# Gated linear attention with a mixer and an MLP on one core: loading two batches in token pairs and replanning the start

## The chip, the cores and the metric

The kernel runs on one core of one Trainium2 chip. The metric is the device time of one execution in microseconds (us); three runs of the kernel before gave 181.0, 179.39 and 182.18 us, a median of 181.0. Lower is better. The core's engines are TensorE (PE in the profile; its weight loads are PEld), VectorE (DVE), ScalarE (ACT), GpSimd (POOL) and SyncE (SP), which here issues every DMA.

## The reference

Two parts follow each other. The first is a recurrence over 768 tokens, for 4 batches and 8 heads of width 48; the second, `_moe_ref`, mixes tokens by a low-rank product and applies an MLP of 384 to 1536 to 384:

```python
def _attn_ref(q, k, v, alpha) -> np.ndarray:
    ...
    for t in range(S):
        state = alpha[:, :, t, :, None] * state + np.einsum('bhd,bhe->bhde', k[:, :, t], v[:, :, t])
        y[:, :, t] = np.einsum('bhd,bhde->bhe', q[:, :, t], state)
    return y.astype(np.float32)
...
    xt = x.transpose(0, 2, 1)
    h = xt @ U @ V
    u = x + h.transpose(0, 2, 1)
    ch = np.maximum(u @ w_ch1, 0.0) @ w_ch2
    return (u + ch).astype(np.float32)
```

x is the recurrence's output with the 8 heads side by side (384 columns). U is 768x32, V 32x768. All inputs and the output are fp32.

## The kernel before, in words

Each batch is cut into six chunks of 128 tokens; a chunk with all 8 heads is called a unit here. A unit needs four loads (alpha, k, q, v), each a tile `io` of 128 tokens x 8 heads x 48 fp32 values, 192 KB. In memory the 48 values of a head and a token stand alone, so such a load consists of pieces of 192 bytes (line 316).

`stage_gla` computes a unit. ScalarE takes the logarithm of alpha (`lt`, line 331). PE sums it over the tokens with a triangular matrix (`f_cum`, 338 to 341), which also gives each column's total. ScalarE exponentiates the sums: `ai` (negative, 349), `aa` (350), `tot` (351). k is multiplied by `ai` (`rk`) and q by `aa` (`rq`, both 356, on VectorE or GpSimd). PE transposes both (368) and an engine copies them out of PSUM as `kt` and `qt` (379, 380). PE forms the scores, two heads at a time on the two halves of its rows (`f_sc`, 389), VectorE masks them (`pm`, 399). `f_d` (414, 416) multiplies `rk` with `rv`, the bf16 copy of v, to the change of the state; `st` is the new state (427, from batch 1 on by way of `sm`, 439). `f_y` (450, 452) adds what the old state and the masked scores give, and a copy writes it to `xb` (458).

`stage_mix` follows when the six chunks of a batch are there: `utx` = x transposed times U (469), its product with V (500) added to x as `ub` (501), and the transposed sum `uT` (488 and 491 in batch 0, 510 later). `mlp1` (537) and `mlp2` (560) are the MLP, 72 matmuls each per batch; `h1t` is the hidden layer after the maximum (547, 549), `ou` the sum that is stored (567, 568). The weights come in 24 loads and are cast to bf16 as `w_sb` (294, 295); rows are whole, 1536 bytes apiece.

The order of all work is made by `Plan.run` before the kernel is built. It keeps a clock for each engine, knows a cost in ns for each operation on each engine that can do it, and takes again and again the operation that can start first; among those that are ready within 1 ns the lowest `prio` wins. For loads it keeps a second clock, `dma`: each load adds its cost there, and its data count as landed 1600 ns later. Buffers come from pools (36 `io` tiles, 8 PSUM banks). An operation of the MLP may take a bank only if `reserve` others are free. The order is then fixed: every engine runs its own list, and an instruction that waits holds up all that stand behind it on that engine. In its early part PE also gets filler matmuls (268) until `warm_until`.

Priorities order the loads: unit number plus 0.0 for alpha, 0.1 for k, 0.2 for q, 1.25 for v (0.3 in the last unit); w1 at 5.5, that is behind the last loads of batch 0, and w2 at 7.9. The call in the last lines is `for b ... for c: st = stage_gla(b, c, st, xb)`, then the mix and the MLP of the batch.

## Time and profile before

| What | Value |
|---|---|
| median of three runs | 181.0 us (179.39 to 182.18) |
| the profiled execution's own time | 180.75 us |
| its span in the profile | 178.9 us |
| mean granted clock of TensorE | 0.981 |
| read from memory, written | 23.79 MB, 4.72 MB |
| DMA packets, those under 512 bytes | 107603, 101408 |

The page gives busy shares of the whole span; the answers by stretch and the timeline give the same for a part. In a timeline row stand the start and the length in us, the engine, the line, the operation with what it writes and reads, and in brackets the idle time of the engine before it with what ended it. In the chain of waits a row is a piece of the path that ended last: start, length, engine and line. A group row ends with its total busy time and the mean ns of one.

### The profile page before, as it was taken

The page shows a single profiled execution, that of the slowest core. Times are in us where ns is not written, and L with a number is a line of the kernel's source. Part 1 is how long each engine was busy: PE and PEld are TensorE (multiplying, and loading weights), DVE is VectorE, ACT ScalarE, POOL GpSimd, SP SyncE. Part 2 cuts the span into 40 slices and gives each one's busy share as a digit, 9 for nine tenths or more (in the row PEclk, how much of TensorE's full clock was granted, in tenths as well). Part 3 has the DMA queues.
Part 4 walks back from the last instruction along what each step waited for, and adds up shares of the span by engine and source line. Part 5 has one row for each costly group of instructions (what it writes and reads, how often), then busy time and mean ns, then how long its engine had stood idle before and what let it go on. Part 6 is the DMA issues. An engine that isn't in the chain of part 4 may idle for free.

```text
span 178.9 us, 4283 instructions
## 1 busy us (share of the span) xinstructions
PE 164.3 (92%) x1622; PEld 101.9 (57%) x1622; DVE 107.4 (60%) x209; ACT 103.0 (58%) x241; POOL 57.1 (32%) x90
## 2 busy tenths in 40 slices
PE   6878797999989997958999999999999999999992
PEld 2344445566557675535766576566664665666660
DVE  2486678888637895873889699386573722100321
ACT  4557366986775546783879758218867200897000
POOL 5432221226334564606673636425600000000000
PEclk9999799999999999996999999999999999999999
DMA  6999999999999999999999999941000023100222
GB/s 122 221 213 191 195 229 302 261 226 292 309 211 196 232 239 223 232 178 196 219 193 200 208 183 234 196 150 48 0 0 4 0 88 129 50 0 0 88 88 88
DMA packets 107603, 28.77 MB, mean 161 GB/s; under 512 B 101408, under 2 KB 107552, under 8 KB 107584
## 3 DMA queue, kind: packets, MB, share of 16 engines
q1 hardware_dynamic: 107584, 28.52, 69.9%
q8 instruction: 12, 0.20, 0.4%
q14 instruction: 7, 0.06, 0.1%
HBM read 23.79 MB, written 4.72 MB: 159 GB/s over the span
## 4 chain that ended last, share of the span: by engine, by line
PE 65%; DVE 7%; DMA 7%; SPq 6%; POOL 5%; issue 5%; ACT 2%; POOLq 0%; DVEq 0%; ACTq 0%
PE ps L560 24%; PE ps L537 21%; SPq L316 6%; PE ps L368 5%; DMA io<-in_q_dram 3%; DVE pm L399 3%; DMA io<-in_moe_w_ch_dram 2%; POOL rk L356 2%; PE ps L389 2%; PE ps L452 2%; POOL rq L356 2%; PE ps L338 2%; DMA out_dram<-ou 2%; PE ps L500 1%; PE ps L450 1%
## 5 line engine op out<-in xcount | busy, mean ns | idle before, releaser
L537 PE MATMUL ps<-uT,w_sb 128*128 128x384 bf16 x288 | 53.8, 332 | 0.4 <-ACT uT L275 0.4
L560 PE MATMUL ps<-w_sb,h1t 128*128 128x384 bf16 x288 | 50.1, 326 | 0.0
L547 ACT ACTIVATE h1t<-ps 128x384 bf16<-128x384 f32 x70 | 33.4, 490 | 21.8 <-PE ps L537 21.4
L560 PEld LDWEIGHTS <-h1t 128*128 128x128 bf16 x288 | 27.1, 98 | 16.5
L537 PEld LDWEIGHTS <-w_sb 128*128 128x128 bf16 x288 | 26.5, 99 | 16.4 <-issue 1.7
L399 DVE TENSOR_TENSOR pm<-ps,maskc 128x512 bf16<-128x512 f32 x48 | 31.0, 683 | 3.2 <-PE ps L389 3.1
L567 DVE TENSOR_TENSOR ou<-ub,ps 128x384 f32<-128x384 bf16 x24 | 13.3, 553 | 32.7 <-PE ps L560 32.6
L356 POOL TENSOR_TENSOR rk<-io,ai 128x384 bf16<-128x384 f32 x21 | 19.5, 928 | 26.1 <-ACT ai L349 25.0
L549 DVE TENSOR_SCALAR h1t<-ps 128x384 bf16<-128x384 f32 x26 | 13.8, 554 | 8.2 <-PE ps L537 8.2
L356 POOL TENSOR_TENSOR rq<-io,aa 128x384 bf16<-128x384 f32 x16 | 14.6, 914 | 8.5 <-ACT tot L351 5.3
L349 ACT ACTIVATE ai<-ps 128x384 bf16<-128x384 f32 x24 | 12.0, 502 | 8.2 <-PE ps L341 7.6
L331 ACT ACTIVATE lt<-io 128x384 bf16<-128x384 f32 x24 | 12.8, 533 | 4.2 <-DMA io<-in_alpha_dram 4.1
L279 POOL CAST rv<-io 128x384 bf16<-128x384 f32 x18 | 9.6, 540 | 11.7 <-DMA io<-in_v_dram 11.7
L268 PE MATMUL ps<-filler 128*128 128x512 bf16 x34 | 12.2, 471 | 1.2 <-DVE offd L235 1.2
L501 DVE TENSOR_TENSOR ub<-xb,ps 128x384 bf16<-128x384 bf16 x24 | 11.6, 547 | 2.6 <-PE ps L500 2.6
L350 ACT ACTIVATE aa<-ps 128x384 bf16<-128x384 f32 x24 | 12.1, 504 | 0.0
L368 PE MATMUL ps<-ident,rq 128*128 128x128 bf16 x96 | 9.4, 220 | 2.3 <-POOL rq L356 2.0
L368 PE MATMUL ps<-ident,rk 128*128 128x128 bf16 x96 | 9.4, 220 | 2.2 <-POOL rk L356 1.3
L275 ACT CAST xb<-ps 128x384 bf16<-128x384 f32 x16 | 7.7, 479 | 6.1 <-PE ps L452 6.0
L427 POOL TENSOR_TENSOR st<-sm,tot 128x384 bf16<-128x384 f32 x8 | 6.6, 828 | 14.3 <-DVE sm L439 14.3
L452 PE MATMUL ps<-rv,pm 128*128 128x48 bf16 x192 | 9.6, 186 | 1.6 <-DVE pm L399 1.6
L275 ACT COPY qt<-ps 128x512 bf16<-128x512 bf16 x12 | 7.1, 588 | 6.2 <-PE ps L368 6.2
(71 smaller groups left out, 198.7 us busy)
## 6 DMA issues: line engine op xcount, KB each, us to landing
io<-in_alpha_dram SPq DMA_DIRECT2D x24, 192.0 KB, 3.8
io<-in_k_dram SPq DMA_DIRECT2D x24, 192.0 KB, 3.9
io<-in_q_dram SPq DMA_DIRECT2D x24, 192.0 KB, 3.7
io<-in_v_dram SPq DMA_DIRECT2D x24, 192.0 KB, 3.7
io<-in_moe_w_ch_dram SPq DMA_DIRECT2D x24, 192.0 KB, 4.7
out_dram<-ou SPq DMA_DIRECT2D x24, 192.0 KB, 1.9
u_in<-in_moe_U_dram SPq DMA_DIRECT2D x1, 96.0 KB, 3.6
v_in<-in_moe_V_dram SPq DMA_DIRECT2D x1, 96.0 KB, 3.3
```

Source lines behind the costliest of these rows:

```text
L268: P.warm = lambda: nc.tensor.matmul(ps[:, 7, :], lhsT=filler[:, 0:128], rhs=filler, start=True, stop=True)
L275: nc.scalar.copy(dst, src)
L331: P.add({"ACT": 435}, lambda e: nc.scalar.activation(lt()[:, :, 0:D], at(), AF.Ln), r=[at], w=[lt], prio=pr + 40, slack=sl)
L356: eng.tensor_tensor(dst()[:, :, 0:D], a(), x(), op=ALU.mult)
L368: nc.tensor.matmul(t[:, p, :], lhsT=ring()[:, 2 * p : 2 * p + 2, :].rearrange("t h w -> t (h w)"), rhs=ident, start=True, stop=True, is_tr ...
L399: nc.vector.tensor_tensor(pm()[:, :, par, :], s2, maskc.to_broadcast([C, HP, C]), op=ALU.mult)
L452: nc.tensor.matmul(y[:, h * D : (h + 1) * D], lhsT=pm()[:, h // 2, h % 2, :], rhs=rv()[:, h, :], start=(h == 0 and sprev is None), stop=(h ...
L537: nc.tensor.matmul(hb()[:, 0:TW], lhsT=w1_sb[:, ct, jt * 128 : (jt + 1) * 128], rhs=uT()[:, ct, tt * TW : (tt + 1) * TW], start=(ct == 0), ...
L547: nc.scalar.activation(dst, hb()[:, 0:TW], AF.Relu)
L549: nc.vector.tensor_scalar_max(dst, hb()[:, 0:TW], 0.0)
L560: nc.tensor.matmul(hb()[:, 0:DM], lhsT=h1()[:, jt, c * C : (c + 1) * C], rhs=w2_sb[:, jt, :], start=(jt == 0), stop=(jt == NJ - 1),)
L567: P.add({"DVE": 468}, lambda e: nc.vector.tensor_tensor(ou(), ub()[:, c, :], hb()[:, 0:DM], op=ALU.add), r=[hb, (ub, c)], w=[ou], prio=-100)
```

## The change

For batches 0 and 1 (`PAIR`) `stage_pair` takes the place of `stage_gla`. A unit there is half of the heads (4) over 256 tokens, with tokens 2p and 2p + 1 in partition p. A load moves the same 192 KB, in pieces of two tokens, 384 bytes. The unit's lower and upper 64 partitions hold 128 consecutive tokens each (c = 0, 1 in the code). The running sums need two more matmuls (`below`, `upto`), since a partition holds an even token and an odd one. Scores, state and output are formed for each half of the partitions alone: 16 score matmuls of 64x128 for 8, 8 state matmuls for 4, 16 output matmuls on 64 rows for 8. State, `sm` and `xb` operations are half as wide and twice as many. The copy to `qt` writes every second element. Two states run side by side, one for each half of the heads.

Alpha's priority is lowered by 0.7, so that it stands ahead of the unit before it in part; in batches 2 and 3 v comes with its unit. The planner takes 750 ns for a paired load and 1000 for another, a landing time of 2000 ns plus 400 for loads, and lets an operation choose only among engines on which it would end within 150 ns of the earliest. Only GpSimd casts w1. Batch 0's `ub` sums are put behind the start of its MLP. The MLP leaves 1 bank free where it left 4. There is a third `aa` and `ai` tile, new constants are made at the start (`upto`, `below`, `mask2`, `maskp`, `onesel`), and fillers end at 28000 ns in the plan.

The core of the diff:

```diff
-    LAT = {"PE": 215.0, "ACT": 155.0, "DVE": 145.0, "POOL": 110.0, "SP": 0.0}
+    LAT = {"PE": 215.0, "ACT": 155.0, "DVE": 145.0, "POOL": 110.0, "SP": 400.0}
     SWITCH = 95.0
+    TOL = 150.0
...
-                for eng in op.engs:
-                    per.setdefault(eng, []).append((max(t, clock.get(eng, 0.0)), op))
+                at = {eng: max(t, clock.get(eng, 0.0)) for eng in op.engs}
+                soon = min(at[eng] + c for eng, c in op.engs.items()) + self.TOL
+                for eng, c in op.engs.items():
+                    if at[eng] + c <= soon:
+                        per.setdefault(eng, []).append((at[eng], op))
...
-                end = dma + 1600.0
+                end = dma + 2000.0
...
+    PAIR = (0, 1)
+    RES = (1, 1, 1, 0)
...
+    upto = const.tile([C, C], BF16, name="upto")
+    nc.vector.tensor_copy(upto, ut_ones)
+    nc.vector.memset(upto[0:64, 64:128], 0.0)
+    below = const.tile([C, C], BF16, name="below")
+    nc.vector.tensor_tensor(below, upto, ident, op=ALU.subtract)
+    mask2 = const.tile([C, 2, 2 * C], BF16, name="mask2")
+    nc.gpsimd.memset(mask2, 0.0)
+    nc.gpsimd.affine_select(
+        out=mask2, in_=mask2, compare_op=ALU.is_gt, fill=1.0, base=0, pattern=[[1, 2], [-1, 2 * C]], channel_multiplier=2
+    )
+    maskp = const.tile([C, 1, 2, C], BF16, name="maskp")
+    nc.vector.tensor_copy(maskp[0:64, 0], mask2[0:64, :, 0:C])
+    nc.vector.tensor_copy(maskp[64:128, 0], mask2[64:128, :, C : 2 * C])
...
-    aas = Pool(slots("aa", 2, [C, H, D], BF16))
-    ais = Pool(slots("ai", 2, [C, H, D], BF16))
+    aas = Pool(slots("aa", 3, [C, H, D], BF16))
+    ais = Pool(slots("ai", 3, [C, H, D], BF16))
...
-    P.warm_until = 33000.0
+    P.warm_until = 28000.0
...
-    def weight(dst, src, key, prio, pr):
+    def weight(dst, src, key, prio, pr, engs):
         t = Buf(io)
-        P.add({"SP": 560.0}, lambda e: nc.sync.dma_start(flat(t), src), w=[t], prio=prio)
-        P.add({"POOL": 485, "ACT": 435}, lambda e: copy(e, dst, flat(t)), r=[t], w=[key], prio=pr)
+        P.add({"SP": 540.0}, lambda e: nc.sync.dma_start(flat(t), src), w=[t], prio=prio)
+        P.add(engs, lambda e: copy(e, dst, flat(t)), r=[t], w=[key], prio=pr)
...
+                weight(w1_sb[:, ct, cs], moe_w_ch1[ct * 128 : (ct + 1) * 128, cs], ("w1", g, ct), 5.5 + 0.01 * g, 560 + g, {"POOL": 485})
...
+            weight(w2_sb[:, jt, :], moe_w_ch2[jt * 128 : (jt + 1) * 128, :], ("w2", jt), W2AT + 0.001 * jt, 700 + jt, {"POOL": 485, "ACT": 435})
...
     def stage_loads(b):
         def load(t, src, c, key):
+            if b in PAIR:
+                hs, sl = slice((c % 2) * HP, (c % 2 + 1) * HP), slice((c // 2) * 2 * C, (c // 2 + 1) * 2 * C)
+                P.add(
+                    {"SP": 750.0},
+                    lambda e: nc.sync.dma_start(
+                        t().rearrange("p (h j) d -> p h (j d)", j=2), src[b, hs, sl, :].rearrange("h (p j) d -> p h (j d)", j=2)
+                    ),
+                    w=[t], prio=key,
+                )
+                return
             sl = slice(c * C, (c + 1) * C)
-            P.add({"SP": 1020.0}, lambda e: nc.sync.dma_start(t(), src[b, :, sl, :].rearrange("h t d -> t h d")), w=[t], prio=key)
+            P.add({"SP": 1000.0}, lambda e: nc.sync.dma_start(t(), src[b, :, sl, :].rearrange("h t d -> t h d")), w=[t], prio=key)
 
         for c in range(NC):
             at, qt, kt, vt = (Buf(io) for _ in range(4))
             tiles[b, c] = at, qt, kt, vt
             kk = b * NC + c
-            for t, src, o in ((at, alpha, 0.0), (kt, k, 0.1), (qt, q, 0.2), (vt, v, 1.25 if c < NC - 1 else 0.3)):
+            for t, src, o in ((at, alpha, -0.7 if c else 0.0), (kt, k, 0.1), (qt, q, 0.2), (vt, v, 1.25 if c < NC - 1 and b in PAIR else 0.3)):
...
+    def stage_pair(b, u, sprev, xb):
+
+        blk, half = u // 2, u % 2
+        pr = (b * NC + u) * 100.0
+        sl = 0.0 if b == 0 else 150.0
+        at, qt, kt, vt = tiles[b, u]
+
+        def raw(t):
+            return t().rearrange("p (h j) d -> p j h d", j=2)
+
+        def jh(x):
+            return x.rearrange("p (j h) d -> p j h d", j=2)
+
+        lt = Buf(lts)
+        P.add({"ACT": 435}, lambda e: nc.scalar.activation(jh(lt()[:, :, 0:D]), raw(at), AF.Ln), r=[at], w=[lt], prio=pr + 40, slack=sl)
+        rv = Buf(rvs)
+        P.add({"POOL": 480, "ACT": 420}, lambda e: copy(e, jh(rv()), raw(vt)), r=[vt], w=[rv], prio=pr + 20, slack=sl)
+
+        cb = Buf(bank)
...
+        def f_cum(e):
+            l2 = jh(lt()[:, :, 0:D])
+            nc.tensor.matmul(cb()[:, 0:DM].rearrange("p (i h d) -> p i h d", i=2, d=D), lhsT=upto, rhs=l2[:, 0:1].to_broadcast([C, 2, HP, D]), start=True, stop=False)
+            nc.tensor.matmul(cb()[:, 0:Q], lhsT=below, rhs=l2[:, 1], start=False, stop=False)
+            nc.tensor.matmul(cb()[:, Q : 2 * Q], lhsT=upto, rhs=l2[:, 1], start=False, stop=False)
+            nc.tensor.matmul(cb()[:, DM : DM + 8], lhsT=ident, rhs=offd.rearrange("p a b -> p (a b)"), start=False, stop=False)
+            tot4 = cb()[:, DM : DM + 8].rearrange("p (c a b) -> p c a b", c=2, a=2)
+            for a in range(2):
+                for j in range(2):
+                    nc.tensor.matmul(
+                        tot4[:, :, a, :], lhsT=lt()[:, HP * j + 2 * a : HP * j + 2 * a + 2, :].rearrange("t h w -> t (h w)"),
+                        rhs=onesel, start=False, stop=(a == 1 and j == 1),
+                    )
+
+        P.add({"PE": mm(DM, Q, Q, 8, 4, 4, 4, 4)}, f_cum, r=[lt], w=[cb], prio=pr + 30, slack=sl)
...
+        rq, rk = Buf(rqs), Buf(rks)
+
+        def f_scale(e, dst, a, x):
+            eng = nc.gpsimd if e == "POOL" else nc.vector
+            eng.tensor_tensor(jh(dst()[:, :, 0:D]), raw(a), jh(x()), op=ALU.mult)
+
+        both = {"DVE": 420, "POOL": 885}
...
+        def f_sc(e):
+            for n in range(4):
+                a, j = n // 2, n % 2
+                for par in range(2):
+                    o = 64 * par
+                    for c in range(2):
+                        r = slice(64 * c, 64 * c + 64)
+                        nc.tensor.matmul(
+                            sc[par]()[r, n * C : (n + 1) * C],
+                            lhsT=kT()[o : o + D, n, r], rhs=qT()[o : o + D, 2 * a + c, :],
+                            start=(n == 0), stop=(n == 3), skip_group_check=True,
+                        )
+
+        P.add({"PE": mm(*[C] * 4)}, f_sc, r=[kT, qT], w=[sc[0], sc[1]], prio=pr + 10, mode="Q", slack=sl)
+
+        def f_mask(par):
+            s2 = sc[par]().rearrange("p (a j c) -> p a j c", a=2, j=2)
...
+        onpe = b == 0
+        nch = 2 if blk < 2 else 1
+        db = [Buf(bank) for _ in range(nch)]
+        st = Buf(sts)
+        before = [(sprev, 1) if sprev is not None else None, (st, 0)]
+
+        def sview(x):
+            return x[0]()[:, 2 * x[1] : 2 * x[1] + 2, :].rearrange("p a d -> p (a d)")
+
+        def f_id(e, c, last):
+            nc.tensor.matmul(db[c]()[:, 0 : 2 * Q // 2], lhsT=ident, rhs=sview(before[c]), start=not last, stop=last, skip_group_check=True)
+
+        def f_d(e):
+            for n in range(4):
+                a, j = n // 2, n % 2
+                for c in range(nch):
+                    r = slice(64 * c, 64 * c + 64)
+                    more = onpe and c == 1
+                    nc.tensor.matmul(
+                        db[c]()[:, a * 2 * D : (a + 1) * 2 * D],
+                        lhsT=rk()[r, HP * j + 2 * a : HP * j + 2 * a + 2, :].rearrange("t h w -> t (h w)"),
+                        rhs=rv()[r, HP * j + 2 * a : HP * j + 2 * a + 2, :].rearrange("t h d -> t (h d)"),
+                        start=(n == 0 and not (onpe and c == 0 and sprev is not None)), stop=(n == 3 and not more), skip_group_check=True,
+                    )
+
+        if onpe and sprev is not None:
+            P.add({"PE": mm(Q)}, lambda e: f_id(e, 0, False), r=[(sprev, 1)], w=[db[0]], prio=pr + 8, slack=sl)
...
+        yb = Buf(bank), Buf(bank)
+
+        def f_yi(e, c):
+            s = before[c]
+            for a in range(2):
+                nc.tensor.matmul(
+                    yb[c]()[:, 2 * a * D : (2 * a + 2) * D], lhsT=qT()[:, 2 * a + c, :], rhs=s[0]()[:, 2 * s[1] + a, :],
+                    start=(a == 0), stop=False, skip_group_check=True,
+                )
+
+        def f_y(e):
+            for c in range(2):
+                if before[c] is not None:
+                    f_yi(e, c)
+            for h in range(HP):
+                for j in range(2):
+                    for c in range(2):
+                        r = slice(64 * c, 64 * c + 64)
+                        nc.tensor.matmul(
+                            yb[c]()[:, h * D : (h + 1) * D], lhsT=pm()[r, (h // 2) * 2 + j, h % 2, :], rhs=rv()[r, HP * j + h, :],
+                            start=(h == 0 and j == 0 and before[c] is None), stop=(h == HP - 1 and j == 1), skip_group_check=True,
+                        )
+
+        P.add({"PE": mm(*[2 * D] * 4, *[D] * 8) + 95}, f_y, r=[qT, rv, (pm, 0), (pm, 1)] + [x for x in before if x is not None], w=[yb[0], yb[1]], prio=pr, mode="H", slack=sl)
+        for c in range(2):
+            P.add({"ACT": 250, "DVE": 265}, lambda e, c=c: copy(e, xb()[:, 2 * blk + c, half * Q : (half + 1) * Q], yb[c]()[:, 0:Q]), r=[yb[c]], w=[(xb, 2 * blk + c, half)], prio=pr, slack=sl)
+        return st
...
-        both = {"DVE": 420, "POOL": 885} if b <= 1 else {"POOL": 885}
+        both = {"POOL": 885}
```

What the planner makes of it is seen in the engines' lists. On SyncE (names: `io` is the tile that a load fills, `in_..._dram` the input), the fourth alpha and what stands around it, before:

```order
L316 DMA io_105<-in_q_dram 128x8x48
L316 DMA io_106<-in_v_dram 128x8x48
L282 DMA u_in<-in_moe_U_dram 128x6x32
L283 DMA v_in<-in_moe_V_dram 32x768
L316 DMA io_107<-in_alpha_dram 128x8x48
L316 DMA io_108<-in_k_dram 128x8x48
```

and now:

```order
L342 DMA io_121<-in_q_dram 128x4x96
L342 DMA io_122<-in_v_dram 128x4x96
L342 DMA io_123<-in_alpha_dram 128x4x96
L305 DMA u_in<-in_moe_U_dram 128x6x32
L306 DMA v_in<-in_moe_V_dram 32x768
L342 DMA io_124<-in_k_dram 128x4x96
```

Alpha went ahead of U and V, and the pieces became 96 values long. Further on SyncE, the end of batch 1's loads and the first stores of results (`out_dram`), before:

```order
L316 DMA io_125<-in_q_dram 128x8x48
L568 DMA out_dram<-ou_194 128x384
L316 DMA io_126<-in_v_dram 128x8x48
L316 DMA io_127<-in_alpha_dram 128x8x48
L316 DMA io_128<-in_k_dram 128x8x48
L568 DMA out_dram<-ou_195 128x384
L316 DMA io_129<-in_q_dram 128x8x48
L316 DMA io_130<-in_v_dram 128x8x48
L316 DMA io_131<-in_v_dram 128x8x48
```

and now, with loads of batch 2 (the rows of line 349) between them:

```order
L342 DMA io_146<-in_v_dram 128x4x96
L342 DMA io_147<-in_v_dram 128x4x96
L349 DMA io_112<-in_alpha_dram 128x8x48
L349 DMA io_113<-in_k_dram 128x8x48
L349 DMA io_114<-in_q_dram 128x8x48
L349 DMA io_115<-in_v_dram 128x8x48
L349 DMA io_119<-in_alpha_dram 128x8x48
L349 DMA io_117<-in_k_dram 128x8x48
L349 DMA io_120<-in_q_dram 128x8x48
L349 DMA io_122<-in_v_dram 128x8x48
L780 DMA out_dram<-ou_213 128x384
```

The first store, which stood six loads ahead of the end of batch 1's, now stands behind two whole units of batch 2. On PE, the running sums of the first unit (`lt` is the logarithm of alpha, `ps` the PSUM), before:

```order
L338 LDWEIGHTS ut_ones
L338 MATMUL ps<-lt_132,ut_ones 128x384
L339 LDWEIGHTS ident
L339 MATMUL ps<-offd,ident 128x8
L341 LDWEIGHTS lt_132
L341 MATMUL ps<-ones,lt_132 128x2
```

and now:

```order
L384 LDWEIGHTS upto
L384 MATMUL ps<-lt_148,upto 128x384
L385 LDWEIGHTS below
L385 MATMUL ps<-lt_148,below 128x192
L386 LDWEIGHTS upto
L386 MATMUL ps<-lt_148,upto 128x192
L387 LDWEIGHTS ident
L387 MATMUL ps<-offd,ident 128x8
```

Two matmuls of 192 columns came in; each piece still loads its own weights.

107 lines of the change are left out of this document (83 added, 24 removed).

## The prediction, on record before the change was timed

> **What bounds the kernel now.** I read the page first, then busy time by stretch, then the chain of waits, then the timeline of the first 35 us. The page has the span and TensorE's share:
>
> ```profile
> span 178.9 us, 4283 instructions
> PE 164.3 (92%) x1622; PEld 101.9 (57%) x1622; DVE 107.4 (60%) x209; ACT 103.0 (58%) x241; POOL 57.1 (32%) x90
> ```
>
> 92% is an average over stretches with different limits. Busy time by stretch (columns: stretch, its length, then PE, PEld, DVE, ACT and POOL busy, PE clock, DMA share, GB/s):
>
> ```profile
> 5.00:15.00 10.00, 8.20 (x101) 4.62 (x99) 6.98 (x14) 5.63 (x16) 4.77 (x6) 1.00 1.09 215
> 15.00:27.00 12.00, 10.04 (x107) 5.11 (x103) 8.96 (x17) 6.72 (x19) 2.41 (x3) 0.86 1.00 205
> 27.00:34.20 7.20, 6.01 (x75) 3.77 (x76) 5.48 (x11) 5.72 (x13) 0.51 (x2) 1.00 0.98 306
> ...
> 70.20:91.00 20.80, 17.39 (x211) 11.60 (x211) 14.68 (x29) 14.89 (x37) 11.36 (x15) 0.92 1.04 213
> 91.00:112.50 21.50, 21.21 (x259) 14.17 (x258) 18.67 (x34) 15.73 (x39) 11.97 (x17) 1.00 1.02 202
> 112.50:175.50 63.00, 62.83 (x498) 38.60 (x496) 23.96 (x46) 28.42 (x61) 7.25 (x10) 1.00 0.19 60
> ```
>
> The DMA engines are full until 112.5 us, and then nearly idle while PE runs alone. So early on loads set the pace, and later PE's backlog does. To size the backlog I price PE's work from the chain of waits (start us, us, what), in its dense parts:
>
> ```profile
> 61.75 0.45 PE ps L368 x8
> ...
> 62.85 0.17 PE ps L416 x4
> 63.02 0.17 PE ps L450 x4
> 63.19 0.20 PE ps L452 x8
> 63.39 0.33 PE ps L389 x8
> 63.72 0.27 PE ps L338
> ...
> 64.09 2.62 PE ps L560 x16
> ```
>
> One unit (128 tokens, all heads) costs 0.45 transposes + 0.17 state + 0.17 and 0.20 output + 0.33 scores + 0.37 running sums (63.72 to 64.09) = 1.69 us. The MLP and the mixer:
>
> ```profile
> 102.12 0.43 PE ps L469 x6
> 103.70 0.97 PE ps L500 x6
> ...
> 112.47 3.90 PE ps L560 x24
> ...
> 140.67 0.34 PE ps L510 x6
> ...
> 152.06 11.70 PE ps L537 x72
> 163.75 11.71 PE ps L560 x72
> 175.49 0.55 DVE ou L567
> ```
>
> An MLP matmul is 11.70/72 = 0.1626 us, a mix 0.43 + 0.97 + 3 x 0.34 = 2.42. From the first L500 of batch 0 (34.16, below) PE owes 576 MLP matmuls (93.7), 18 units (30.4, less 1.0 for the missing first and last state pieces), 0.97 and three mixes (7.3): **131.3 us**. It takes 175.49 - 34.16 = 141.3, so 10.0 us are not work. Check: from 112.47 the order holds 332 MLP matmuls (54.0) and 8.3 of other pieces, 62.3 in 63.0 us: 1.2% over. The rest of the 10.0 lies mostly in 70.2 to 91, where PE's queue stood behind late loads:
>
> ```profile
> 80.50 0.51 POOL L279 CAST rv<-io 128x384 bf16<-128x384 f32 x1 [4.73 <-DMA io<-in_v_dram]
> 81.06 0.44 PE L416 MATMUL ps<-rv,rk 128*128 128x96 bf16 x4 [2.02 <-POOL rv L279]
> ```
>
> So: front 34.2 + work 131.3 + waits 10.0 + end 3.4 (175.49 to 178.9), and 1.85 around the span, is 180.75, the profiled execution's time. The median shown is 181.0, so nothing has to be scaled.
>
> **Loads.** A 196,608-byte load at 215 and 205 GB/s takes 0.91 and 0.96 us, say 0.94; this is 1024 packets of 192 B on 16 engines, 14.7 ns each. The stretch of weight loads (306 GB/s, 1536-B packets) gives 0.64 us a load, 80 ns a packet. The line through both is 5.3 ns + 0.049 ns a byte: a 384-B packet takes 24.1 ns and a load of 512 of them 0.77 us, 0.17 saved (an estimate). Bounds: 0.94 if time goes by bytes, 0.47 if by packets. I take 0.77, the nearest the rows allow. 24 loads save 4.1 us, all 48 save 8.2. The Trainium skill ("DMA: Bandwidth & Descriptors", Specifications) gives 512 B as the least transfer for full rate; by it 384 B stays in the penalised class. That is the third rival below.
>
> **Front.** The rows are of the last unit of batch 0, and of the load two units earlier:
>
> ```profile
> 12.62 5.37 DMA io<-in_q_dram
> ```
> ```profile
> 26.84 0.90 DVE L356 TENSOR_TENSOR rq<-io,aa 128x384 bf16<-128x384 f32 x1
> 29.53 1.28 DVE L399 TENSOR_TENSOR pm<-ps,maskc 128x512 bf16<-128x512 f32 x2
> 30.87 0.35 PE L452 MATMUL ps<-rv,pm 128*128 128x48 bf16 x7 [0.40 <-DVE pm L399]
> 34.16 1.14 PE L500 MATMUL ps<-utx,vm_sb 128*128 128x384 bf16 x6
> ```
>
> The fourth q landed at 12.62 + 5.37 = 17.99; the sixth comes 8 loads later, 25.5. In the change 22 loads stand up to it, so it lands 22 x 0.17 = 3.7 earlier, at 21.8. With alpha sent a unit ahead, its decay factors are ready by then, where before rq began at 26.84, 1.3 after q. From rq to the end of the output is 26.84 to 31.22 = 4.4, with the strided copy 0.1 more: 26.4; and 2.9 from there to 34.16: MLP start 29.3. VectorE is the doubt. Its forms now (mean ns):
>
> ```profile
> L399 DVE TENSOR_TENSOR pm<-ps,maskc 128x512 bf16<-128x512 f32 x48 | 31.0, 683 | 3.2 <-PE ps L389 3.1
> L356 DVE TENSOR_TENSOR rq<-io,aa 128x384 bf16<-128x384 f32 x8 | 6.7, 832 | 0.3 <-issue 0.3
> L277 DVE COPY kt<-ps 128x512 bf16<-128x512 bf16 x13 | 5.5, 424 | 2.7 <-PE ps L368 2.2
> L427 DVE TENSOR_TENSOR st<-ps,tot 128x384 bf16<-128x384 f32 x8 | 4.4, 553 | 2.0 <-PE ps L416 1.9
> L356 DVE TENSOR_TENSOR rk<-io,ai 128x384 bf16<-128x384 f32 x3 | 1.7, 558 | 5.5 <-ACT ai L349 5.5
> ```
>
> Up to batch 0's last output it now holds 12 pm (7.7 at the 0.64 spacing of the 1.28 row), 8 rk or rq (4.5 to 6.7), 3 copies (1.3), 15 half-width st and xb (between 4.1 at half of 553 and 8.3 at all of it): 17.6 to 24.0 in the 21 us from 5.3. At the lower half that is about 90% full, so I add 0.9: MLP start 30.2, **-4.0**. The extra constants on VectorE and GpSimd (small memsets, a 128x512 mask) run before the first load's factors are wanted and cost 0 to 0.5 there, hidden by the later loads.
>
> **PE work.** Per paired unit: the running sums get 384 more columns (+0.16, by the MLP matmul). Output matmuls go from 8 to 16 on half the rows; the 8 of L452 take 0.20, 25 ns each, so +0.20. Scores: 16 small ones at 25 ns are 0.40 against 0.33, +0.07; upper end, 16 at the 41 ns of the present 8, +0.33. State 8 for 4, +0.03, upper +0.17. Sum +0.46, between 0.16 and 0.86; six units of batch 1: **+2.8** (1.0 to 5.2). Those of batch 0 lie in the front, under the loads. L469 shows that matmuls on column strips do run together: six of 384 columns in 0.43, where L500's six take 0.97. The Trainium skill ("TensorEngine Tiling (Array Packing)", Restrictions and Gotchas) says that column tiling gives up fast weight loading; by it the scores, with 16 weight loads, go to the upper end, and the sum would be 1.6 us more. L469 has only six loads behind long matmuls and can't show it.
>
> **Waits.** Three rows place the DMA limit:
>
> ```profile
> 55.38 2.20 SPq L568 DMA_DIRECT2D out_dram<-ou  x1
> 65.64 1.28 POOL L279 CAST rv<-io 128x384 bf16<-128x384 f32 x2
> 75.94 0.33 PE L416 MATMUL ps<-rv,rk 128*128 128x96 bf16 x4
> ```
>
> Batch 1's last v are there by 65.64. Less 8.2 for 48 loads and 1.3 for two stores that the order now places later, 56.1; four loads of batch 2 (3.8) and a cast (0.5): its first state matmul, at 75.94 before, can run at about 60.5 to 61. (SyncE also stood 2.20 us at a store amid batch 1's loads; the first store now follows them.) PE gets there at 30.2 + 134.1 - 104.5 (work still left there: 44 + 432 MLP matmuls 77.4, three mixes 7.3, the other pieces 19.8) = 59.8, so it loses about 1 us, and then runs on backlog: 61 + 104.5 x 1.012 + 1 + 3.4 + 1.85 = 173.0, a second way to nearly the same time. Waits: 1.2% of 134.1 (1.6), 0.8 at that point, 2 for the other engines in the denser 30 to 75 us: 4.4 for 10.0, **-5.6**. GpSimd alone casting w1 costs 12 x 0.51:
>
> ```profile
> L279 POOL CAST w_sb<-io 128x384 bf16<-128x384 f32 x9 | 4.6, 511 | 10.6 <-DMA io<-in_moe_w_ch_dram 10.4
> L275 ACT CAST w_sb<-io 128x384 bf16<-128x384 f32 x15 | 7.5, 512 | 2.8 <-DMA io<-in_moe_w_ch_dram 2.8
> ```
>
> That is under the 0.64 at which they land, so nothing; what queues behind is batch 1's first rv cast, whose v lands after the last w1 anyway. The choice by end time changes engines, not the amount of work: 0, with +-1 in the range.
>
> **Sum:** 180.75 - 4.0 + 2.8 - 5.6 = 174.0.
>
> **Rivals.** (1) *VectorE becomes the front's limit*: at its upper 24.0 the last pm ends at 29.3, the output 0.4 later and the MLP starts at 32.6; then 32.6 + 134.1 x 1.012 + 2 + 5.25 = 175.6. For: 90% full already. Against: half-width should cost about half. (2) *Half-array matmuls don't overlap*: outputs too at 41 ns (+0.46), all upper ends, 1.1 a unit: 6.7 for 2.8, 177.9, less the 0.8 that PE waits anyway: 177. Against: L389's two halves overlap today. (3) *A 384-B packet costs by its bytes*, the page's rule: no load is shorter, the front has only the fuller VectorE (+0.8), the 10.0 of waits stay, the work is 2.8 more: 184; with the stores' 1.3 and the earlier order 181. Slower. It decides if a paired load takes over 0.9. Against: weight packets run at 306 GB/s, so some cost is per packet. (4) *In-order queues*: the rewritten order holds PE behind one late engine after another and the waits stay 10.0: 179.6. For: DVE, ACT and POOL together are busy 41 of 62 us in 70 to 91 already.
>
> **Chances.** Forecast 0.52 (own range 171 to 176.5), (1) 0.10, (2) 0.12, (3) 0.11, (4) 0.15. A measurement here tells 2% from no change: 177.4 and 184.6. Faster: forecast, (1) and nearly half of (2), 0.67; slower: the upper half of (3) and mishaps, 0.09; same 0.24. The range 170 to 181.5 leaves out most of (3) and a quicker packet.
>
> **What would show it.** Paired loads at 250 GB/s or more in 5 to 20 us (step 1; 215 would be rival 3); the first MLP matmul at 29 to 31; VectorE at 9 tenths before; a paired unit 0.4 to 0.5 dearer on PE; the first state matmul of batch 2 near 61; no slice of 70 to 91 with PE under 9 tenths; the last load landing near 106 and PE dense from 62. Wrong if the MLP starts after 33, or PE waits over 7 us behind that.

## The result, and the profile after

The changed kernel takes **174.5 us** (median of 4 runs, 173.7 to 175.4) against 181.5 for the kernel before in the same comparison (179.4 to 182.2): a ratio of 0.966, 95% interval 0.955 to 0.976. Ratios here and below leave out runs over 1.5% above the fastest of the same kernel, so they are not quite the quotients of the medians. The prediction was 174.0, in a range of 170 to 181.5, with "faster" at 0.67. Time and direction are right. Of the reasons one is missing, and the experiments found it.

The profiled execution took 174.75 us. Its page:

```profile
span 173.0 us, 4823 instructions
...
PE 161.9 (94%) x1862; PEld 104.2 (60%) x1862; DVE 109.0 (63%) x232; ACT 104.1 (60%) x247; POOL 59.5 (34%) x97
```

PE has 240 more instructions in a span that is 5.9 us shorter, and its share goes from 92 to 94%. Busy time by stretch (stretch, its length, PE, PEld, DVE, ACT, POOL, PE clock, DMA share, GB/s):

```profile
5.00:15.00 10.00, 8.26 (x145) 5.30 (x144) 7.57 (x24) 7.97 (x20) 3.60 (x6) 1.00 1.21 262
15.00:27.00 12.00, 10.90 (x212) 7.88 (x212) 9.53 (x22) 8.52 (x23) 6.88 (x11) 0.86 1.04 270
...
50.00:55.00 5.00, 3.54 (x56) 2.52 (x55) 3.83 (x12) 3.15 (x9) 1.42 (x2) 1.00 1.04 232
55.00:90.00 35.00, 35.00 (x466) 23.70 (x463) 27.88 (x56) 24.84 (x60) 17.33 (x23) 1.00 1.03 204
90.00:110.00 20.00, 19.37 (x222) 13.01 (x221) 13.71 (x27) 12.96 (x34) 9.13 (x13) 1.00 1.19 206
110.00:169.50 59.50, 59.50 (x495) 37.14 (x492) 25.55 (x47) 28.26 (x61) 6.63 (x8) 1.00 0.14 48
```

In the front the loads now run at 262 and 270 GB/s (215 and 205 before). From 55 us PE is full, where before 70 to 91 was the thin stretch (17.39 of 20.80); what is left of the waits shows at 50 to 55. The first mixer and MLP matmuls, and the last sum, on the timelines of PE and VectorE:

```profile
30.53 0.33 PE L712 MATMUL ps<-utx,vm_sb 128*128 128x384 bf16 x1
30.69 1.14 PE L749 MATMUL ps<-uT,w_sb 128*128 128x384 bf16 x6
```
```profile
169.54 0.55 DVE L779 TENSOR_TENSOR ou<-ub,ps 128x384 f32<-128x384 bf16 x1 [1.40 <-PE ps L772]
```

So the front ends at 30.5 (34.2 before), 139.0 us follow to the last sum (141.3), then 3.5 of span and 1.75 around it.

Two of the three longest waits of PE behind the front, on the timelines of PE, GpSimd, ScalarE and PE again:

```profile
54.01 0.35 PE L479 MATMUL ps<-rv,rk 64*128 64x96 bf16 x8 [1.46 <-POOL rv L302]
```
```profile
53.45 0.50 POOL L302 CAST rv<-io 128x384 bf16<-128x384 f32 x1 [1.72 <-DMA io<-in_v_dram]
```
```profile
90.41 0.52 ACT L547 ACTIVATE lt<-io 128x384 bf16<-128x384 f32 x1 [1.40 <-DMA io<-in_alpha_dram]
```
```profile
91.46 0.40 PE L605 MATMUL ps<-qt,kt 48*128 48x128 bf16 x8 [0.63 <-ACT qt L298]
```

In the first, a state matmul of batch 1 stands in PE's queue until a v has landed and been cast. In the second ScalarE waits for an alpha, and PE waits 0.63 us for the qt copy queued behind it.

### The profile page after: what moved, and what is told of

It is laid out like the page before. It is cut to its first block, busy times and chain, and to the rows that moved or that the text cites. A ratio compares the mean times of both kernels' runs of the same rounds, so it can differ in the third digit from the quotient of the medians.

```text
span 173.0 us, 4823 instructions
## 1 busy us (share of the span) xinstructions
PE 161.9 (94%) x1862; PEld 104.2 (60%) x1862; DVE 109.0 (63%) x232; ACT 104.1 (60%) x247; POOL 59.5 (34%) x97
## 4 chain that ended last, share of the span: by engine, by line
PE 60%; DMA 19%; SPq 15%; issue 2%; POOL 1%; ACT 1%; DVE 0%; ACTq 0%; POOLq 0%
PE ps L772 27%; PE ps L749 16%; SPq L342 10%; DMA io<-in_v_dram 8%; DMA io<-in_moe_w_ch_dram 5%; SPq L317 3%; DMA io<-in_alpha_dram 3%; PE ps L584 3%; DMA io<-in_k_dram 3%; PE ps L605 2%; PE ps L712 2%; PE ps L722 2%; PE ps L664 1%; PE ps L554 1%; PE ps L418 1%
## 5 line engine op out<-in xcount | busy, mean ns | idle before, releaser
L749 PE MATMUL ps<-uT,w_sb 128*128 128x384 bf16 x288 | 53.1, 326 | 0.0
L772 PE MATMUL ps<-w_sb,h1t 128*128 128x384 bf16 x288 | 52.8, 326 | 0.0
L772 PEld LDWEIGHTS <-h1t 128*128 128x128 bf16 x288 | 26.1, 98 | 16.0 <-issue 1.0
L749 PEld LDWEIGHTS <-w_sb 128*128 128x128 bf16 x288 | 26.1, 98 | 15.4
L615 DVE TENSOR_TENSOR pm<-ps,maskc 128x512 bf16<-128x512 f32 x24 | 15.7, 685 | 6.7 <-PE ps L605 6.5
L572 POOL TENSOR_TENSOR rk<-io,ai 128x384 bf16<-128x384 f32 x12 | 11.0, 916 | 20.2 <-ACT ai L565 18.7
L456 DVE TENSOR_TENSOR pm<-ps,maskp 128x512 bf16<-128x512 f32 x24 | 15.8, 681 | 0.7 <-ACT h1t L759 0.5
L298 ACT CAST xb<-ps 128x192 bf16<-128x192 f32 (+1 forms) x23 | 8.8, 392 | 11.6 <-PE ps L664 7.6
L298 ACT COPY kt<-ps 128x512 bf16<-128x512 bf16 x17 | 10.0, 586 | 5.8 <-PE ps L584 5.3
L298 ACT COPY qt<-ps 128x512 bf16<-128x512 bf16 x17 | 11.3, 663 | 1.6 <-PE ps L418 1.0
L302 POOL CAST w_sb<-io 128x384 bf16<-128x384 f32 x21 | 10.8, 527 | 3.8 <-DMA io<-in_moe_w_ch_dram 3.5
L572 POOL TENSOR_TENSOR rq<-io,aa 128x384 bf16<-128x384 f32 x12 | 11.6, 967 | 0.0
L298 ACT COPY uT<-ps 128x768 bf16<-128x768 bf16 x4 | 3.2, 799 | 8.6 <-PE ps L722 5.1
```

What stands on the lines that cost most here:

```text
L298: nc.scalar.copy(dst, src)
L302: nc.gpsimd.tensor_copy(dst, src)
L456: nc.vector.tensor_tensor(dst, s2, maskp.to_broadcast([C, 2, 2, C]), op=ALU.mult)
L572: eng.tensor_tensor(dst()[:, :, 0:D], a(), x(), op=ALU.mult)
L615: nc.vector.tensor_tensor(pm()[:, :, par, :], s2, maskc.to_broadcast([C, HP, C]), op=ALU.mult)
L749: nc.tensor.matmul(hb()[:, 0:TW], lhsT=w1_sb[:, ct, jt * 128 : (jt + 1) * 128], rhs=uT()[:, ct, tt * TW : (tt + 1) * TW], start=(ct == 0), ...
```

## The experiments

Twelve kernels ran, in four sets, each set on one chip beside runs of the kernel before, whose median in these sets was 183.3 to 183.5. Ratios are against those. `first MLP` is the start of the first L749 (L753 where the code has 4 more lines) in the profile.

| kernel | median us | ratio | 95% interval | first MLP |
|---|---|---|---|---|
| the change, again | 176.8 | 0.965 | 0.958 to 0.971 | 29.8 |
| short pieces | 191.7 | 1.047 | 1.040 to 1.054 | 38.7 |
| no pairs | 184.8 | 1.010 | 1.006 to 1.015 | 35.8 |
| pairs only | 188.0 | 1.026 | 1.019 to 1.032 | 37.7 |
| pairs in batch 0 alone | 177.7 | 0.970 | 0.964 to 0.975 | 30.0 |
| masks later | 176.1 | 0.958 | 0.949 to 0.967 | 30.4 |
| alpha not ahead | 177.0 | 0.965 | 0.959 to 0.971 | 33.1 |
| no choice by end time | 176.3 | 0.965 | 0.958 to 0.972 | 30.3 |
| w1 cast by two engines | 176.2 | 0.958 | 0.950 to 0.967 | 34.5 |
| old load numbers | 176.3 | 0.960 | 0.953 to 0.967 | 30.6 |
| old bank rules | 186.3 | 1.018 | 1.013 to 1.022 | 33.9 |
| old reserve alone | 186.1 | 1.024 | 1.018 to 1.031 | 33.4 |

**Is it the length of the pieces?** The same lists, counts and order of instructions, but each token of a pair gets its own place in the tile, so that a paired load is 1024 pieces of 192 B:

```diff
-t().rearrange("p (h j) d -> p h (j d)", j=2), src[b, hs, sl, :].rearrange("h (p j) d -> p h (j d)", j=2)
+t().rearrange("p (j h) d -> p j h d", j=2), src[b, hs, sl, :].rearrange("h (p j) d -> p j h d", j=2)
```

> The changed kernel with one thing undone: the paired loads of batches 0 and 1 go to memory in pieces of 192 bytes again (1024 packets a load instead of 512); every engine's list of instructions stays as it is, in the same order. Theory A (the shorter loads carry the gain): a load takes 0.93 to 0.96 us instead of 0.74, so the last load that TensorE waits for (its output at 54.0 us in the changed kernel) comes about 40 loads x 0.2 = 8 us later; start of the MLP at 33 to 35 instead of 30.5; time 181 to 184, ratio to before about 1.00 to 1.01. Theory B (the new order and choice of engines carry it, the loads were hidden): MLP start within 1 us of 30.5, time up to 177, ratio under 0.98.

> The changed kernel itself, beside the three others on the same chip: 173.5 to 175.5, ratio 0.955 to 0.975. It gives the base for differences under 1%.

191.7 us: slower than the kernel before, as the first theory says, and by more than it said. Loads by stretch, first of the short pieces, then of the change again and of the kernel without pairs, all on the same chip:

```profile
5.00:15.00 10.00, 7.13 (x92) 4.26 (x91) 5.69 (x19) 6.21 (x16) 1.55 (x3) 0.94 1.31 191
15.00:30.00 15.00, 13.99 (x205) 9.44 (x205) 9.27 (x20) 9.03 (x24) 5.34 (x8) 0.50 1.02 178
```
```profile
5.00:15.00 10.00, 8.86 (x145) 5.44 (x144) 7.56 (x24) 7.99 (x20) 3.58 (x6) 1.00 1.18 255
```
```profile
5.00:15.00 10.00, 8.05 (x83) 4.08 (x82) 8.54 (x24) 5.27 (x14) 0.00 (x0) 1.00 1.43 190
```

191 GB/s against 255: 1.03 us a load against 0.77. The layout of the copies differs a little too, but the kernel without pairs, whose pieces are also 192 B, reads 190 GB/s in this stretch on this chip. So the piece length sets the rate. The MLP starts 8.9 us later than with long pieces, and 14.9 us are lost in all. TensorE's granted clock was 0.50 from 15 to 30 us; how much of the loss is that, no run separates.

**What does the plan do without pairs?** All the planner's new numbers and rules are kept, and both batches are loaded and computed as before:

```diff
-    PAIR = (0, 1)
+    PAIR = ()
...
-            for t, src, o in (..., (vt, v, 1.25 if c < NC - 1 and b in PAIR else 0.3)):
+            for t, src, o in (..., (vt, v, 1.25 if c < NC - 1 and b < 2 else 0.3)):
...
-        both = {"POOL": 885}
+        both = {"DVE": 420, "POOL": 885} if b <= 1 else {"POOL": 885}
...
```

> The changed kernel without pairs: batches 0 and 1 in units of 128 tokens and 8 heads as before, while the planner's new load costs, the choice of engines by end time, alpha a unit ahead, w1 on GpSimd, the late ub sums and the bank rule stay. Theory A: the loads are long again and the gain is gone but for the order's own part: MLP start 33 to 35, waits on loads between 70 and 91 us back, time 179 to 182.5. Theory B: 174 to 177, like the changed kernel or better, since the paired units' extra matmuls (some 2 us) are gone.

184.8, 1% above the kernel before, and above what either theory allowed. The planner's part alone gives nothing.

**What do pairs do without the plan?** The pairs are kept, and the planner's numbers and rules are those of before (the list is in the expectation):

> Batches 0 and 1 in token pairs, as in the changed kernel, under the planner's numbers and rules of the kernel before (no landing latency, load costs 1020 and 560, no choice by end time, alpha not ahead, warm-up planned to 33 us, the old reserves of PSUM banks, w1 cast by GpSimd or ScalarE, v late in every batch). Theory A (the shorter packets' count is the gain, and the plan only follows): 173.5 to 177, ratio 0.955 to 0.975 against before, first MLP matmul at 29.5 to 31.5. Theory B (the pairs pay only with the plan made for them): 178 to 182, ratio 0.98 to 1.00, since in-order queues with the old order wait for loads at other places; then PE would show more than 9 us of waits after its first MLP matmul, or that matmul would come after 32.

188.0: 2.6% *slower* than the kernel before, and beyond the 182 of the second theory. Neither part pays alone. From the diff:

```diff
-    LAT = {..., "SP": 400.0}
+    LAT = {..., "SP": 0.0}
-    TOL = 150.0
+    TOL = 1e9
-    RES = (1, 1, 1, 0)
+    RES = (4, 4, 4, 0)
...
-            pr = mlp_prio(0, 0.3)
+            pr += 100.0
-            hb = Buf(bank, 3 if b == 0 else 0)
+            hb = Buf(bank)
```

I first blamed landing times: in this profile PE waits 1.27 us, until 58.5, for a 0.91 us GpSimd multiply that stands behind two casts of late v. The next runs took most of the planner's edits back one at a time, with the pairs in place. Not undone by themselves were the end of the fillers, the place of v in batches 2 and 3, and the third `aa` and `ai` tiles.

**Four edits whose undoing shows in no time.** Alpha ahead, the choice by end time, the casts of w1, the load numbers:

```diff
-(at, alpha, -0.7 if c else 0.0)
+(at, alpha, 0.0)
```
```diff
-    TOL = 150.0
+    TOL = 1e9
```
```diff
-560 + g, {"POOL": 485})
+560 + g, {"POOL": 485, "ACT": 435})
```
```diff
-    LAT = {..., "SP": 400.0}          # and: end = dma + 2000.0; costs 450, 500, 540, 1000
+    LAT = {..., "SP": 0.0}            # and: end = dma + 1600.0; costs 620, 250, 560, 1020
```

> The changed kernel with alpha back at its own unit's place in the load queue (offset 0.0 for all units); the plan is made anew, and the w1 loads and alphas of 50 to 70 us change places. Theory A (where loads are the limit, at the v of batch 1 near 54 us, a queue that is full gives the same bytes in any order): 174.5 to 177.5, within 1% of the changed kernel. Theory B (alpha's lead is what lets ScalarE start each unit early, as the waits ACT lt <- alpha of 31.8 and 90.4 us suggest): 178 to 180, with ACT waiting for alpha at more places.

> The changed kernel with the choice of engine by earliest start, as before (no end-time rule). Theory A (the step of my sum that gave it 0 +-1): 175 to 178, first MLP matmul 29.5 to 31.5. Theory B (the rule keeps 0.7 to 0.9 us GpSimd multiplies out of the front, where they would end later than on VectorE): first MLP matmul at 32 to 34 and 178 to 180.

> The changed kernel with the casts of w1 again open to ScalarE as well as GpSimd. Theory A (casts cost nothing on GpSimd, which is idle a third of that stretch): 175.5 to 177.5, the same within 0.7%. Theory B (the casts on ScalarE hold lt and the exponentials back by 0.4 to 0.5 us each in 50 to 70 us): 177.5 to 179, with PE slices under 9 tenths in 55 to 70 us.

> The changed kernel (pairs, bank rules, choice by end time, alpha ahead, w1 on GpSimd), with the planner's numbers for loads alone as in the kernel before: no landing latency (0 in place of 400, +1600 in place of +2000), whole loads 1020, w loads 560, u and v 620 and 250. Theory T (with pairs alone the time was 5 to 11 us above the changed kernel because the plan takes loads to land about 0.8 us earlier than they do, so instructions are queued ahead of their data on in-order engines): 180 to 186, ratio 0.98 to 1.01, with PE waits at 50 to 60 us over 2 us. Theory U (the numbers of the loads do little, the reserves of PSUM banks and the place of ub did it): 175 to 178.5, ratio 0.955 to 0.975.

Ratios 0.958 to 0.965, all within the interval of the change itself, so none of the four is shown to be worth anything, with room for 1 to 2% either way; and the landing-time theory (T in the last of these) falls.

Two of these kernels start the MLP 3 to 5 us later and still end with the others. Without alpha's lead it is mostly a matter of order: batch 1's first sums, which wait 1.71 us for ScalarE's `lt`, stand ahead of the first MLP matmul, and in the change again the same sums wait 1.48 us behind six of these. With w1 cast by two engines the delay is real. On ScalarE's timeline, then on PE's:

```profile
29.46 1.03 ACT L298 CAST w_sb<-io 128x384 bf16<-128x384 f32 x2 [2.17 <-DMA io<-in_moe_w_ch_dram]
30.40 0.31 ACT L298 CAST xb<-ps 128x192 bf16<-128x192 f32 x1
```
```profile
30.76 0.50 PE L681 MATMUL ps<-xb,u_sb 128*32 128x384 bf16 x2 [3.27 <-ACT xb L298]
```

Two casts that wait for w1 hold up batch 0's last `xb` copy on ScalarE, and PE stands idle for 3.27 us. Yet from its first L712 at 34.14 to its last sum at 172.50 PE is then idle for only 1.4 us, where the change again is idle for 5.3 (29.67 to 171.78). What the front loses the waits behind it give back, so here a microsecond of the front isn't a microsecond of the end. This is one profile, its run, at 177.7, is the slowest of four, and the orders differ behind the front too.

**The bank rules.** First all of them, then the MLP's reserve alone:

```diff
-    RES = (1, 1, 1, 0)
+    RES = (4, 4, 4, 0)
-            pr = mlp_prio(0, 0.3)
+            pr += 100.0
-            hb = Buf(bank, 3 if b == 0 else 0)
+            hb = Buf(bank)
```
```diff
-    RES = (1, 1, 1, 0)
+    RES = (4, 4, 4, 0)
```

> The changed kernel with the reserves of PSUM banks (4 in place of 1, none for ub) and the place of ub as in the kernel before, and the load numbers of the changed kernel. Theory T (load times in the plan are what counts): 175 to 178.5, ratio 0.955 to 0.975. Theory U (with 4 banks in reserve the MLP can't fill PE while loads are late): 181 to 187, ratio 0.985 to 1.02, with PE under 8 tenths at 50 to 60 or 100 to 110 us, and the MLP's work left to the end.

> The changed kernel with one part of the bank rules undone: the MLP of batches 0 to 2 again takes a PSUM bank only when 4 others are free (1 in the changed kernel). The place and the reserve of batch 0's ub sums stay as changed. With all the bank rules undone the time was 186.3. Theory R (the reserve is the cause: a paired unit takes 9 banks in turn where a block took 7, and with 4 held back the MLP is kept out of the stretch in which units run): 183 to 187, ratio 0.995 to 1.02; MLP matmuls (of w1 and of w2) hold under 20 us of PE before 75 us, against 26.6 in the changed kernel. Theory S (the place of the ub sums is the cause: six of them and their VectorE sums stood ahead of the first MLP matmul and held back the next unit): 175 to 178.5, ratio 0.955 to 0.975, with 25 us or more of MLP on PE before 75 us.

186.3 and 186.1: with the pairs in place, one number moves the time by some 6% (ratio 1.024 against 0.965), and the bank rules alone account for most of what the pairs lose under the old plan (1.018 against 1.026). The orders of these two kernels come out the same but for the place of one matmul of L712, so they serve as one experiment done twice, and the place of the `ub` sums is not what costs the time here; whether it matters with a reserve of 1 was not run. MLP matmuls on PE, by stretch (columns as above; only PE and PEld are of that line): of the changed kernel L749, then L772; then the same two of the old reserve:

```profile
30.00:75.00 45.00, 14.21 (x72) 6.27 (x72) 1.00 1.03 244
```
```profile
30.00:75.00 45.00, 12.08 (x60) 5.01 (x60) 1.00 1.03 244
```
```profile
30.00:75.00 45.00, 14.66 (x72) 6.22 (x72) 0.96 1.06 239
```
```profile
30.00:75.00 45.00, 4.79 (x27) 2.56 (x28) 0.96 1.06 239
```

132 MLP matmuls (26.3 us) lie before 75 us in the change, 99 (19.5 us) with the old reserve. The rest comes at the end, where nothing else is left to do. The last pieces of the chain of waits, first of the change, then of the old reserve:

```profile
143.50 2.60 PE ps L772 x16
146.10 11.70 PE ps L749 x72
157.80 11.71 PE ps L772 x72
```
```profile
146.46 11.05 PE ps L772 x68
157.51 11.70 PE ps L749 x72
169.21 11.71 PE ps L772 x72
```

So 212 MLP matmuls run alone at the end where 160 did. The 52 more, at 0.1626 us each, are 8.5 us of the 9.3 between the two kernels (the change again ends with 160 as well).

Early on, PE's list has no MLP matmul ahead of a unit that is late; on the timeline of PE with the old reserve:

```profile
30.70 0.98 PE L712 MATMUL ps<-utx,vm_sb 128*128 128x384 bf16 x5
...
46.09 0.40 PE L418 MATMUL ps<-ident,rk 128*128 128x128 bf16 x4 [2.41 <-DVE rk L405]
```

The kernel before also holds 4 banks back, and runs all 144 MLP matmuls of batch 0 before 75 us (26.0 us: 12.86 + 13.17), as does the kernel without pairs with the new reserve (26.7 us: 13.51 + 13.18). So a reserve of 4 did not keep batch 0's MLP out where units are whole; more this count can't show, since no other MLP work was ready by then, and a kernel without pairs in which the reserve alone differs was not run. A reason offers itself in the code: a block takes 7 banks in turn (running sums, two transposes, two scores, state, output), a paired unit 9, since state and output are two each in the first four units. That this count is the reason was not tried by itself.

**Which batch pays?** Pairs in batch 0 alone:

```diff
-    PAIR = (0, 1)
+    PAIR = (0,)
```

> The changed kernel with pairs in batch 0 alone; batch 1 is loaded and computed as in the kernel before, with whole-block loads at 1000 in the plan. It parts the terms of my sum: the front (-3.6 measured) hangs on batch 0, the waits after it on the loads of both. Theory A (terms as they stand: front kept; PE work +0.75 in place of +1.5; 24 loads of 0.25 us, 6 us of transfer, come back, against which 3.8 us fewer waits were measured): MLP start 29.5 to 31.5, 177 to 181, ratio 0.965 to 0.985. Theory B (the front alone pays, batch 1 is hidden behind its MLP work anyway): 174 to 176.5, ratio 0.95 to 0.965.

177.7, as the first theory has it: ratio 0.970 (0.964 to 0.975), next to 0.965 (0.958 to 0.971) with both: batch 0 brings nearly all of the gain, and what batch 1 adds can't be told from nothing.

**Constants.** The masks are made after the other constants, so that VectorE and GpSimd reach `offd`, which PE waits for, sooner:

```diff
     maskp = const.tile([C, 1, 2, C], BF16, name="maskp")
-    nc.gpsimd.memset(mask2, 0.0)
-    nc.gpsimd.affine_select(...)
-    nc.vector.tensor_copy(maskp[0:64, 0], mask2[0:64, :, 0:C])
-    nc.vector.tensor_copy(maskp[64:128, 0], mask2[64:128, :, C : 2 * C])
...
     for x in rq_s:
         nc.gpsimd.memset(x[:, :, D:], 0.0)
+    nc.gpsimd.memset(mask2, 0.0)
+    nc.gpsimd.affine_select(...)
+    nc.vector.tensor_copy(maskp[0:64, 0], mask2[0:64, :, 0:C])
+    nc.vector.tensor_copy(maskp[64:128, 0], mask2[64:128, :, C : 2 * C])
```

> The changed kernel with the mask of the paired units (GpSimd's memset and select, VectorE's two copies of 1.10 and 0.23 us) made after the other constants. In the changed kernel the first running sums wait for these copies and the first ai stands at 5.57 us, 0.75 later than before. Theory A (loads set the pace to 54 us): first ai at 4.8 to 4.9, MLP start at most 0.4 earlier, time within 0.4 of the changed kernel. Rival C (the front is a chain of engine work, loads wait for it): MLP start 0.6 to 0.8 earlier and time 0.5 to 0.8 lower.

The first `ai` starts at 5.14 us instead of 5.57 (4.82 in the kernel before), and the MLP at 30.4, no earlier than in the change again (29.8). The time, 176.1 against 176.8, doesn't tell. Its ratio and those of the two other kernels near 0.958 to 0.960 overlap with the change's own; none is shown to beat it.

## Why the prediction was right, and where its steps were not

**The sum.** The four terms, against the first profile of the change (work 131.3 as before, plus the price of pairs):

| term | predicted | measured |
|---|---|---|
| front | -4.0 | -3.6 (34.16 to 30.53) |
| PE work | +2.8 | +1.5 |
| waits | -5.6 (to 4.4) | -3.8 (139.0 - 132.8 = 6.2) |
| whole | 174.0 | 180.75 - 3.6 + 1.5 - 3.8 = 174.85; 174.75 was timed |

An error of 1.3 in the work and one of 1.8 in the waits cancel. The same kernel on another chip has 142.1 us where 139.0 stand here (29.67 to 171.78 from the first L712, against 30.53 to 169.54), so the waits are known no better than 3.1 us, and the agreement to half a microsecond is partly luck.

The waits of this sum are also a remainder, time less priced work. PE's own idle time, from the first mixer matmul to the last sum, before, in the change and with the old reserve:

```profile
34.16:175.49 141.33, 136.52 (x1333) 87.16 (x1331) 84.49 (x158) 82.94 (x195) 47.06 (x65) 0.99 0.65 149
```
```profile
30.53:169.54 139.01, 136.11 (x1461) 87.81 (x1459) 87.35 (x173) 84.24 (x200) 43.08 (x59) 1.00 0.68 150
```
```profile
30.70:180.95 150.25, 139.70 (x1461) 88.40 (x1459) 85.86 (x168) 85.18 (x202) 43.70 (x62) 0.99 0.63 140
```

Length less busy time is 4.8, 2.9 and 10.6 us, and 5.3 in the change again. So of the 10.0 us called waits before, about half was idle time; the other half is time that counts as busy but that the priced work does not fill. Idle time fell by 1.9 of the 3.8 in one profile and not at all in the other.

**Loads: right.** 262 and 270 GB/s are 0.75 and 0.73 us a load, where 0.77 was taken between bounds of 0.47 and 0.94. The third rival, that a 384-B packet costs by its bytes, is out, with the 181 us that it gave. The trace speaks against the rule of the Trainium skill that was named beside it ("DMA: Bandwidth & Descriptors", Specifications: 512 B as the least transfer for full rate) only as far as it is read as a step: a 384-B piece does stay under the rate of the weight loads, but lies far above the 192-B one (306 GB/s for the weights, 262 and 270 for 384 B, 215 and 205 for 192 B). That a piece under the least length costs by its bytes was my own reading; no price stands there.

**Front: right in size, by other limits.** The last q was put at 21.8 and the last `rq` right behind it, with the decay factors ready by then. They were not: ScalarE waited for the last alpha until 19.90, and `aa` ended at 22.75 (22.27 + 0.48).

```profile
19.90 0.52 ACT L375 ACTIVATE lt<-io 128x384 bf16<-128x384 f32 x1 [0.36 <-DMA io<-in_alpha_dram]
22.27 0.48 ACT L399 ACTIVATE aa<-ps 128x384 bf16<-128x384 f32 x1
```

VectorE, busy with other work, began `rq` at 23.29:

```profile
22.28 0.72 DVE L300 COPY qt<-ps 128x512 bf16<-128x512 bf16 x1
22.90 0.34 DVE L300 CAST xb<-ps 128x192 bf16<-128x192 f32 x1
23.29 0.56 DVE L405 TENSOR_TENSOR rq<-io,aa 128x384 bf16<-128x384 f32 x1
```

So of the 1.5 us about 1.0 is the late factor and 0.5 VectorE. The 0.9 us that the sum put on for a full VectorE covers most of it by luck. VectorE itself was less busy than the 9 tenths foretold: 17.1 of the 22 us from 5 to 27. The half-width forms took 0.35 us (the lower end was half of 0.553, 0.28), which leaves the first rival's 24.0 far off.

**Constants: wrong, and harmless.** "0 to 0.5, hidden" was 0.75: the first `ai` came at 5.57 for 4.82. One copy of the mask took 1.10 us on VectorE. The run with the masks later got back 0.43 of it, and no time that could be told.

**PE's price: the term was sized twice too large.** On the chain of waits of the change:

```profile
54.69 0.16 PE ps L384
54.85 0.08 PE ps L385
54.93 0.08 PE ps L386
55.02 0.10 PE ps L391 x4
...
56.24 0.35 PE ps L445 x16
...
58.99 0.17 PE ps L518 x4
59.16 0.30 PE ps L531 x16
59.46 0.17 PE ps L479 x4
```

Running sums 0.43 (0.37 before), 16 scores 0.35 (0.33; 0.40 to 0.66 was allowed), outputs 0.17 + 0.30 (0.17 + 0.20; +0.20 was taken), state 0.17 as before, or 0.27 for the eight of an early unit, by the spacing on the timeline:

```profile
46.84 0.34 PE L479 MATMUL ps<-rv,rk 64*128 64x96 bf16 x8
47.11 0.66 PE L749 MATMUL ps<-uT,w_sb 128*128 128x384 bf16 x3
```

That is +0.18 for two units of a batch and +0.28 for four: 1.5 where 2.8 stood. Matmuls on half and quarter arrays overlap: 16 scores take 22 ns each where the second rival's upper end had 41, and it is out. The 16 weight loads cost the scores 0.02 us. The Trainium skill ("TensorEngine Tiling (Array Packing)", Restrictions and Gotchas) says that column tiling excludes fast weight load; a loss from that, which the prediction held possible, does not show here.

**Waits: 1.8 off in size, and the reason was half of it.** "-5.6" was worked out from shorter loads and moved stores, with PE running on MLP backlog meanwhile. With the pairs, that backlog is there because the MLP's reserve went from 4 banks to 1, an edit which the sum never priced. With the old reserve, the waits are 180.95 - 30.70 - 132.8 = 17.4 us instead of falling (10.6 of them idle, at most 1.8 the lower clock, 0.96 over 45 us), and the fourth rival, in-order queues that keep their waits, wins by more than it claimed. This is the step that failed: but for 2 us, the loads were taken as the only thing that could keep PE idle, and the banks of a paired unit were not counted. Had the reserve stayed at 4, the time would have been about 185.9 (1.024 x 181.5), 12 us above 174.0.

**Front plus waits: added as if they did not touch.** The run with w1 on two engines started its MLP 4.6 us later than the change again and ended within 0.7 us of it, with 3.9 us less idle time behind the front. A gain in the front is in part taken back by the next wait that the loads set.

**The place of the limit: wrong.** Batch 2's first state matmul was to meet the loads at 60.5 to 61. It ran at 63.8, behind PE's own work, and the last load-bound wait of that part was one batch earlier, at 54.0, for a v of batch 1. On the chain of waits:

```profile
47.36 6.04 DMA io<-in_v_dram
...
54.01 0.35 PE ps L479 x8
...
63.80 0.17 PE ps L628 x4
```

From 55 to 90 us PE is full, as forecast for 70 to 91 (34.2 of 35 in the change again). The loads end at about 109 to 110, not 106 (the DMA share falls from 1.19 to 0.14 at 110).

**w1, end time, alpha.** The first two were priced at nothing within 1 us. The runs that undid them agree in time, though w1 on two engines costs 3.3 us in the front. Alpha's lead was part of the front's account; without it the time is the same.

## What to carry to other kernels

When an edit makes work finer, count what it holds as well as what it costs: here an early unit takes two PSUM banks more, the likely reason why the old reserve then kept the filler work off TensorE, so that the faster loads alone made the kernel slower. Undo each edit of a bundle with the rest in place, since a part that gives nothing alone may be what the others stand on. And where two halves of a sum come out wrong in opposite directions, a right total confirms neither. Check a term called waits against the idle time itself, and ask of two terms whether a gain in one is taken back by the other.

## What the runs showed of the hardware

- Loads of 192 KB in 192-B pieces ran at 190 and 191 GB/s in two kernels, and in 384-B pieces at 255, on one chip in the same stretch. In the first two profiles the same stretch has 215 and 262. Doubling the piece is worth a fifth to a third more, although 512 packets remain.
- A copy of a PSUM tile that writes every second bf16 element costs more than the 0.1 us that the prediction put on: on VectorE 0.72 us (22.28 above) against 0.42 for the plain one, on ScalarE 0.74 against 0.59, as its timeline in the front of the change shows:

```profile
12.00 0.74 ACT L298 COPY qt<-ps 128x512 bf16<-128x512 bf16 x1
12.66 0.59 ACT L298 COPY kt<-ps 128x512 bf16<-128x512 bf16 x1
```

- One small mask copy took over four times as long as its twin (groups by form):

```profile
L244 DVE COPY maskp<-mask 64x256 bf16<-64x256 bf16 x1 | 1.1, 1097 | 0.9 <-POOL mask L240 0.9
L245 DVE COPY maskp<-mask 64x256 bf16<-64x256 bf16 x1 | 0.2, 230 | 0.0
```

  GpSimd was at its own constants during the long one. In the run with the masks later it had one copy of 0.29 us left to do, and the same VectorE copy took 0.28 us. So the copy by itself is not long; that GpSimd's work makes it so is argued from this.
- With short pieces TensorE ran at a granted clock of 0.50 for 15 us of the front, and the mean clock of all four runs was 0.92 to 0.94, where the change has 0.98 to 1.00. Shorter dips come and go: from 15 to 27 us the change shows 0.86 in one profile and 1.00 in the other, of the same instructions in the same order. What lowers the clock stays open.
